# Scores of two pairs of heads in seven shared blocks, heads A and B on the two halves of TensorE's rows, and softmax's division moved to the output

## The chip, the cores and the metric

The kernel runs on one core of a Trainium2 chip. The metric is device microseconds of one execution, smaller is better. The core's engines are TensorE (PE; its weight loads stand apart as PEld), VectorE (DVE), ScalarE (ACT), GpSimd (POOL) and SyncE (SP, which here only issues DMAs). PSUM has eight banks of 128 x 512 f32.

## The reference, cut to what matters

Attention over 8 batches of 12 heads (448 tokens, 64 numbers each), then a gated MLP over each batch:

```
q_n, k_n = rmsnorm(q, g_q), rmsnorm(k, g_k)
scores   = (q_n @ k_n.T) / 8                 # 448 x 448 per head
attn     = exp(scores - max);  attn /= sum(attn) + 1e-9
x        = attn @ v                          # heads beside each other: 448 x 768 per batch
h        = gelu(x @ w_in);  u, w = halves of h
out      = x + (u * (w_sg @ layernorm(w) + b_sg)) @ w_out
```

All inputs are float32 or float64. The kernel gets float32 precision out of 16-bit matmuls: it splits each operand into a high float16 part and a low one (what the high part leaves over) and adds up the products of the parts.

## The kernel before, in words

The work goes through 48 pairs of heads, A and B (six pairs a batch). A pair has 2 x 448 = 896 rows of scores in seven tiles of 128 rows by 448 keys. Three tiles are A's, three are B's, and the middle one holds 64 rows of each.

For each pair: `load_qk` brings q and k of two pairs by eight DMAs, on ACT's queue (L269). `squares` (ACT square L324, DVE sum L325) and `norms` (DVE, small operands, L335 and L107 to L118) make the RMS factors. `split` multiplies by them on POOL (L344, L345), takes the high part on ACT (L347) and the low one on POOL (L348), copies k's parts with high and low swapped (DVE L350, L351), and one DMA transpose (SP, L352) makes `qt`. In `qt` the 128 partitions are 64 high and 64 low numbers of one head, so two matmuls with all 128 rows of TensorE (L411) give high x high + low x low, and high x low + low x high.

`scores` then does, for each tile: the maximum (DVE L414) on the scores in a PSUM bank; the exponential (ACT L416) from PSUM into a float32 tile `a` in SBUF, which also sums the row; for every two or three tiles a scale and a reciprocal of the sums (DVE L420, L422); the high part of `a` times the reciprocal on POOL (L430, three tiles of seven, four in the first batch) or ACT (L432, the rest); the low part on DVE (L433); and, for two tiles at a time, a DMA transpose into `at` (SP, L436). A PSUM bank of scores is free as soon as L416 has read it; there are four of them (NS), and three for the MLP (NM) and one for pv (NV).

`vsplit` makes v's high and low part (ACT L384, DVE L386), `vsquares` the sums for v's scale (ACT L367). `pv` of the pair before multiplies (L453 for 384 query columns, L455 for the other 64): A's matmuls use columns 0 to 63 of TensorE and B's columns 64 to 127. Eleven steps of four matmuls, then `xh` (ACT L461) and `xl` (DVE L462). `moe` is the MLP of the batch before: L517 and L520 (v half), L575 (u half), L605 (over tokens), L639 to L651 (output); gelus stand in clusters between two loads of ACT's table (L471, L480). The output goes out on ACT's queue (L658 to L661).

The order on each engine is set at build time: the main loop (L709 to L764) takes steps of `scores`, `pv`, the weights and `moe` in turn, and a list scheduler places the instructions by priority. Engines take their instructions in that order.

Of the kernel before, what the change touches and what calls it, by code (L numbers as in the profile page):

```python
# [44 lines left out]
def kernel(  # L45
# [28 lines left out]
    C7 = 2 * CM + 1  # L74
    EH = DM // 2
# [34 lines left out]
    def newton(y, x, t):  # L110
        """y, a guess of x ** -0.5 within 3.5%, made better by a step of third and one of second order."""
# [41 lines left out]
    def weights():  # L153
        nonlocal mlp
        ctx_w = ExitStack()
        # w_in's parts take the place of its float32 values, one K block after the other
# [49 lines left out]
        for c in range(CM):  # L206
            nc.sync.dma_start(out=wsr[c], in_=w_sg[0:SM].rearrange("(p c) s -> p c s", c=CM)[:, c])
# [489 lines left out]
    for i in range(NG):  # L697
        squares(i)
        norms(i, 1)
        if i == 0:  # L700
            split(0, V)
# [94 lines left out]
```

## Time and profile before

| | |
|---|---|
| Time, three runs | 1047.78, 1049.43 (median), 1049.59 us |
| Profiled execution, first to last instruction (span) | 1047.2 us; 2.2 us under the median |
| Busy: DVE, PE, ACT, POOL | 899.9, 809.6, 705.4, 504.6 us |
| The same as shares of the span | 86%, 77%, 67%, 48% |
| Mean granted clock of TensorE | 0.903 of full speed |
| DMA packets, bytes | 528217, 177.74 MB |

A row of the groups view reads: line of the kernel, engine, operation, tile written <- tiles read, shape (partitions x elements), count | busy time of the group in us, mean ns of one | idle time of the engine just before them and what ended it. Busy time of a group is the time in which at least one of them ran, so matmuls, which overlap, have a sum of means above their busy time. "PE s L411 <- ACT a L416: 63.5, 40, 7.9" in the view of waits says that L411 waited 63.5 us in 40 waits, 7.9 the longest, and that L416 ended those waits. In a timeline row the first number is the start in us, the second the length. Profile lines before carry line numbers of the kernel before.

### The profile page before, as it was taken

What the parts mean: (1) busy time and instruction counts of PE and PEld (TensorE: products, weight loads), DVE (VectorE), ACT (ScalarE), POOL (GpSimd) and SP (SyncE); (2) the same over time, 40 slices, a digit from 0 to 9 for tenths busy, and PEclk for the clock granted to TensorE, in tenths of its full rate; (3) what the DMA queues carried; (4) which work ended last, traced back from release to release, by engine and by line L of the source; (5) the groups of instructions that cost most, each with busy time, mean ns of one, the idle gap of its engine ahead of it and who ended that gap; (6) DMA issues with size and microseconds to landing.
All of it is one profiled execution on the core that took longest, in us unless ns stands there. A gap on an engine that the chain in (4) does not pass through costs nothing. (4 is left out here: it accounts for less than half of the span.)

```text
span 1047.2 us, 17092 instructions
## 1 busy us (share of the span) xinstructions
PE 809.6 (77%) x5652; PEld 447.3 (43%) x5652; DVE 899.9 (86%) x1959; ACT 705.4 (67%) x1418; POOL 504.6 (48%) x435
## 2 busy tenths in 40 slices
PE   0333556757689798888979899887979799799998
PEld 0111222424454346444644357343634365346546
DVE  4999979999789997999979998999889988999430
ACT  2565787676677777677767767587667686877441
POOL 1777745637536463443545372545455443535021
PEclk9666688888899899899999899999989999999999
DMA  5969589685989979996797879994989779838501
GB/s 144 254 174 244 125 179 215 160 185 108 207 180 206 194 156 206 173 217 152 162 213 181 167 149 196 202 211 106 207 190 195 148 166 201 180 89 174 110 1 61
DMA packets 528217, 177.74 MB, mean 170 GB/s; under 512 B 472257, under 2 KB 521985, under 8 KB 528129
## 3 DMA queue, kind: packets, MB, share of 16 engines
q1 hardware_dynamic: 484928, 144.07, 66.6%
q10 hardware_dynamic: 43200, 32.59, 11.3%
q8 instruction: 44, 0.72, 0.3%
q14 instruction: 45, 0.36, 0.1%
HBM read 54.58 MB, written 11.01 MB: 63 GB/s over the span
## 5 line engine op out<-in xcount | busy, mean ns | idle before, releaser
L433 DVE SCALAR_TENSOR_TENSOR ahl<-a,rc,ahl 128x448 f16<-128x448 f32 x336 | 289.6, 886 | 32.1 <-POOL ahl L430 22.0
L416 ACT ACTIVATE a<-s,nm 128x448 f32<-128x448 f32 x336 | 211.0, 630 | 124.7 <-DVE ahl L433 78.0
L411 PE MATMUL s<-qt 128*128 128x448 f16 (+1 forms) x768 | 192.2, 388 | 120.8 <-ACT a L416 63.5
L430 POOL TENSOR_SCALAR ahl<-a,rc 128x448 f16<-128x448 f32 x150 | 117.3, 786 | 230.0 <-DVE rc L422 99.9
L414 DVE TENSOR_REDUCE nm<-s 128x1 f32<-128x448 f32 x336 | 200.2, 610 | 18.5 <-PE s L411 18.0
L432 ACT ACTIVATE ahl<-a,rc 128x448 f16<-128x448 f32 x186 | 118.1, 662 | 61.5 <-DVE rc L422 34.2
L411 PEld LDWEIGHTS <-qt 128*128 128x128 f16 (+1 forms) x768 | 57.2, 105 | 209.2 <-issue 127.8
L345 POOL TENSOR_TENSOR qk<-qk,ny 128x896 f32<-128x896 f32 x47 | 83.2, 1792 | 70.6 <-DVE ny L118 34.4
L348 POOL TENSOR_TENSOR hl<-qk,hl 128x896 f16<-128x896 f32 x47 | 95.7, 2037 | 34.4 <-ACT hl L347 26.3
L453 PE MATMUL pv<-at,vl 128*64 128x384 f16 x384 | 68.2, 368 | 56.7 <-DMA at<-ahl 44.8
L344 POOL TENSOR_TENSOR qk<-qk,gg 128x448 f32<-128x448 f32 x47 | 58.9, 1255 | 77.0 <-ACT sqk L324 76.8
L453 PE MATMUL pv<-at,vh 128*64 128x384 f16 x672 | 91.0, 357 | 0.0
L575 PEld LDWEIGHTS <-wi 128*128 128x128 f16 x576 | 57.4, 102 | 61.8 <-issue 15.9
L455 PE MATMUL pv<-at,vh 128*64 128x64 f16 x672 | 78.7, 202 | 0.0
L611 POOL TENSOR_TENSOR gt<-gt,u 128x448 f32<-128x448 f32 x32 | 39.0, 1221 | 79.0 <-DVE gt L610 59.2
L453 PEld LDWEIGHTS <-vl 128*64 128x64 f16 x384 | 30.7, 118 | 90.0 <-DMA at<-ahl 37.0
L416 ACT ACTIVATION_READ_ACCUMULATOR a<-s,nm 128x1 f32 x336 | 65.9, 196 | 0.0
L325 DVE TENSOR_REDUCE ss<-sqk 128x14 f32<-128x896 f32 x48 | 51.5, 1073 | 15.5 <-ACT sqk L324 15.2
L347 ACT ACTIVATE hl<-qk 128x896 f16<-128x896 f32 x48 | 45.3, 945 | 25.6 <-DMA qk<-in_k_dram 11.4
L324 ACT ACTIVATE sqk<-qk 128x896 f32<-128x896 f32 x48 | 45.3, 944 | 21.7 <-DVE ss L325 11.2
L453 PEld LDWEIGHTS <-vh 128*64 128x64 f16 x672 | 50.2, 120 | 18.6 <-issue 0.8
L420 DVE TENSOR_SCALAR rc<-sums 128x2 f32<-128x2 f32 x144 | 52.1, 364 | 7.1 <-ACT a L416 6.5
(995 smaller groups left out, 2096.0 us busy)
## 6 DMA issues: line engine op xcount, KB each, us to landing
qk<-in_k_dram ACTq DMA_DIRECT2D x48, 192.0 KB, 3.6
vr<-in_v_dram SPq DMA_DIRECT2D x16, 576.0 KB, 4.9
vr<-in_v_dram SPq DMA_DIRECT2D x32, 288.0 KB, 5.9
out_dram<-ot ACTq DMA_DIRECT2D x24, 384.0 KB, 3.8
qk<-in_q_dram ACTq DMA_DIRECT2D x46, 192.0 KB, 3.6
raw<-in_moe_w_in_dram SPq DMA_DIRECT2D x12, 512.0 KB, 4.9
vr<-in_v_dram SPq DMA_DIRECT2D x32, 96.0 KB, 4.9
at<-ahl SPq DMA_TRANSPOSE x192, 3.8
```

The costliest lines, as they stand in the source:

```text
L344: E.tensor_tensor(out=qk[:, C7:], in0=qk[:, C7:], in1=gg.unsqueeze(1).broadcast_to([P, C7, D]), op=ALU.mult)
L345: E.tensor_tensor(out=qk, in0=qk, in1=r["rs"].unsqueeze(2).broadcast_to([P, SSW, D]), op=ALU.mult)
L348: E.tensor_tensor(out=hl[:, 0:SSW, 1], in0=qk, in1=hl[:, 0:SSW, 0], op=ALU.subtract)
L411: mm(out=ps[p0:p1], lhsT=qt[:, t * P + p0:t * P + p1], rhs=qt[:, k0:k0 + S], start=(n == 0), stop=(n == 1))
L414: V.tensor_reduce(out=nm, in_=ps, axis=AX.X, op=ALU.max, negate=True)
L416: A.activation(out=a, in_=ps, func=AF.Exp, bias=nm, accum_out=sums[:, t - t0:t - t0 + 1])
L430: G.tensor_scalar(out=hl[:, 0], in0=a, scalar1=sc, scalar2=1.0, op0=ALU.mult, op1=ALU.mult)
L432: A.activation(out=hl[:, 0], in_=a, func=AF.Copy, scale=sc)
L433: V.scalar_tensor_tensor(out=hl[:, 1], in0=a, scalar=sc, in1=hl[:, 0], op0=ALU.mult, op1=ALU.subtract)
L453: mm(out=o[:, 0:SM].rearrange("p (c n) -> p c n", c=CM), lhsT=w, rhs=at[:, h * CK:h * CK + CM, blk], start=(n == 0), stop=(n == n_s - 1), ...
L455: mm(out=o[:, SM:S], lhsT=w, rhs=at[:, CM, blk, h * HP:(h + 1) * HP], start=False, stop=(n == n_s - 1), skip_group_check=True)
L575: done = mm(out=ps[:, 0:S], lhsT=ww[:, g, f * P:(f + 1) * P], rhs=xx, start=(n == 0), stop=(n == 17))
```

## The change: what it does

The unit of the scores is now two pairs of heads (24 units). Tokens are laid out so that seven blocks of 128 rows hold both pairs: blocks 0 to 2 and the lower half of block 3 are pair 0, the rest is pair 1. A block has 64 numbers of head A beside 64 of head B; q's high, q's low, k's high and k's low part are four such sets. After the transposes (two per unit, q and k apart) A's numbers lie on partitions 0 to 63 and B's on 64 to 127. A tile of scores is 128 rows of both heads: A's matmuls take the lower half of TensorE's rows into one PSUM bank and B's the upper half into a second, three products each (high x high, low x high, high x low). So a unit has 7 tiles of 896 numbers a row, 168 in all, where there were 336 of 448.

Per tile there is one maximum over both banks (L392), two exponentials that write back into PSUM (L394), one high part for both heads on ACT (L397, none on POOL), one low part on DVE (L398), both read from PSUM, and one DMA transpose (L403; two of 64 rows where the ring of `at` wraps). The two banks are free only after L398; there are two such pairs of banks (NS = 2). The parts are no longer divided by the sum. Instead `recips` (per pair) adds 1e-9 on POOL, takes the reciprocal on DVE, splits it on POOL, spreads it over 64 partitions by 16 small matmuls against an identity (L423), copies that out on ACT (L426); and `pv` multiplies its output by it on DVE (L450). `pv` has twelve steps of two matmuls over all 448 columns. v is loaded without its duplicates. All loads of q and k and the output's stores are on SP's queue now, in halves of 64 partitions. In the last batch's MLP two tiles of the v half go block by block along with the heads, where it was three.

```diff
-RG = ((0, 2), (2, 4), (4, 7))
-TG = (2, 2, 2, 1)
-PT, PT0 = (0, 3, 6), (0, 2, 4, 6)
...
-NS, NV, NM = 4, 1, 3
...
-NA, NAH, NAT, NQT, NVH, HLB = 4, 4, 2, 2, 2, 2
+NS, NV, NM = 2, 1, 3
...
+NAT, NAH, NQT, NVH, HLB, GV = 3, 3, 2, 2, 3, 3
...
-        qs = qs or [nc.scalar]
+        qs = qs or [nc.sync]
...
+        qk = ld.tile([P, 2, 2, C7, D], F32, name="qk", bufs=NQK)
         for x, src in enumerate((q, k)):
...
+            for half, j, b0, c0, n in ((lo, 0, 0, 0, C4), (hi, 0, 0, C4, CM), (lo, 1, C4, C4, CM), (hi, 1, CM, 0, C4)):
+                qs[nq % len(qs)].dma_start(
...
-    def split(i, E=G):
...
-        V.tensor_copy(out=hl[:, SSW:, 0], in_=hl[:, C7:SSW, 1])
-        V.tensor_copy(out=hl[:, SSW:, 1], in_=hl[:, C7:SSW, 0])
-        r["tr"] = nc.sync.dma_start_transpose(out=qt, in_=hl.rearrange("p c x d -> p (c x d)"))
...
+    def split(u, E=G):
...
+        qt = att.tile([P, 4, C7 * P], F16, name="qt", bufs=NQT)
+        for x in range(2):
...
+            A.activation(out=h_, in_=r["qk"][:, x], func=AF.Copy)
+            E.tensor_tensor(out=l_, in0=r["qk"][:, x], in1=h_, op=ALU.subtract)
+            r["tr"] = nc.sync.dma_start_transpose(
...
-    def scores(i):
...
-                for n in range(2):
-                    for p0, p1, h in parts:
-                        k0 = (2 * (n + 1) + h) * S
-                        mm(out=ps[p0:p1], lhsT=qt[:, t * P + p0:t * P + p1], rhs=qt[:, k0:k0 + S],
-                           start=(n == 0), stop=(n == 1))
...
-                A.activation(out=a, in_=ps, func=AF.Exp, bias=nm, accum_out=sums[:, t - t0:t - t0 + 1])
...
+    def scores(u):
...
+        for t in range(C7):
+            ps = ps_s.tile([P, 2, 512], F32, name="s")
+
+            rows = [(slice(0, P), t // C4)] if t != CM else [(lo, 0), (hi, 1)]
+            for m, (qx, kx) in enumerate(((0, 2), (1, 2), (0, 3))):
+                for h in range(2):
+                    hs = slice(h * HP, (h + 1) * HP)
+                    for r_, j in rows:
+                        mm(out=ps[r_, h, 0:S], lhsT=qt[hs, qx, t * P + r_.start:t * P + r_.stop],
+                           rhs=qt[hs, kx, j * S:(j + 1) * S], start=(m == 0), stop=(m == 2))
+            nm = sml.tile([P, 2], F32, name="nm", bufs=6)
+            V.tensor_reduce(out=nm, in_=ps[:, :, 0:S], axis=AX.X, op=ALU.max, negate=True)
+            for h in range(2):
+                A.activation(out=ps[:, h, 0:S], in_=ps[:, h, 0:S], func=AF.Exp, bias=nm[:, h:h + 1], accum_out=sums[:, t, h:h + 1])
+            yield
+            ahl = att.tile([P, 2, 2, S], F16, name="ahl", bufs=NAH)
+            A.activation(out=ahl[:, 0], in_=ps[:, :, 0:S], func=AF.Copy)
+            V.tensor_tensor(out=ahl[:, 1], in0=ps[:, :, 0:S], in1=ahl[:, 0], op=ALU.subtract)
...
+    def recips(i):
...
+        G.tensor_scalar(out=x, in0=sums, scalar1=1e-9, scalar2=None, op0=ALU.add)
+        V.reciprocal(out=y, in_=x)
+        G.tensor_copy(out=rh, in_=y)
+        G.tensor_tensor(out=rl, in0=y, in1=rh, op=ALU.subtract)
...
+                    mm(out=ps[h * HP:(h + 1) * HP, o:o + w], lhsT=rx[ks, 2 * n + h:2 * n + h + 1].broadcast_to([w, HP]),
+                       rhs=ident_h[ks, ks], start=(n == 0 and rx is rh), stop=(n == CM and rx is rl), skip_group_check=True)
+        row = att.tile([P, S], F32, name="row", bufs=1)
+        A.activation(out=row, in_=ps, func=AF.Copy)
...
+        for k_, (vx, n, hx) in enumerate(blocks):
+            for h, (ks, c) in enumerate(hx):
+                mm(out=ps[h * HP:(h + 1) * HP], lhsT=vx[ks, c], rhs=at_all[ks, n + c, o:o + S],
...
+        V.tensor_tensor(out=ps, in0=ps, in1=row, op=ALU.mult)
...
-                nc.scalar.dma_start(out=om[t], in_=ot)
...
+            for h in range(2):
+                nc.sync.dma_start(out=om[1][t + h * C4] if t < CM else om[h][CM], in_=ot[h * HP:(h + 1) * HP])
```

On ACT, a stretch in a middle batch of the kernel before, while the MLP's gated tiles (`gh`) are made: `a` is an exponential, `ahl` the high part; "waits" names the engines whose semaphores the instruction waits for.

```order
L416 ACTIVATE a_5528,sums_5501<-s_5523,nm_5526 128x448 [waits DVE_49]
L612 ACTIVATE gh_5329<-gt_5401 128x448 [waits Pool_49]
L416 ACTIVATE a_5606,sums_5599<-s_5601,nm_5604 128x448 [waits DVE_49]
L416 ACTIVATE a_5627,sums_5599<-s_5620,nm_5625 128x448 [waits DVE_49,PE_49]
L432 ACTIVATE ahl_5573<-a_5528,rc_5502 128x448 [waits DMAHW5_49,DVE_49,Activation_49]
L432 ACTIVATE ahl_5638<-a_5606,rc_5600 128x448 [waits DMAHW6_49,DVE_49,Activation_49]
L416 ACTIVATE a_5673,sums_5666<-s_5668,nm_5671 128x448 [waits DVE_49]
```

The same place in the changed kernel: `s` is the pair of banks, written back by its two exponentials.

```order
L394 ACTIVATE s_5956,sums_5802<-s_5956,nm_5963 128x448 [waits DVE_49]
L369 ACTIVATE vh_6065<-vr_5248,v_s_5409 128x448 [waits PE_49]
L394 ACTIVATE s_5956,sums_5802<-s_5956,nm_5963 128x448 [waits Activation_49]
L453 ACTIVATE xh_6029<-pv_5897 128x448 [waits DVE_49]
L397 ACTIVATE ahl_5987<-s_5956 128x896 [waits DMAHW3_49,Activation_49]
L605 ACTIVATE gh_6147<-gt_6235 128x448 [waits Pool_49]
L394 ACTIVATE s_5999,sums_5802<-s_5999,nm_6012 128x448 [waits DVE_49]
```

Before, ACT waits for DVE ahead of an exponential and the high parts lag; now a tile's two exponentials and its high part stand close together, and the second exponential and the high part wait for ACT's own earlier work.

On SP, the DMAs of about a pair and a half of heads in the kernel before (`vr` is v, `at` the transposed weights of attention, `qt` the transposed q and k), all transposes but for the end of a load of v:

```order
L307 DMA vr_4260<-in_v_dram 64x6x64 [waits DMAHW5_49]
L307 DMA vr_4260<-in_v_dram 64x6x64 [waits DMAHW6_49]
L436 DMA_TRANSPOSE at_4271<-ahl_4323 128x14x128 [waits DMAHW2_49,DVE_49,DMAHW7_49,PE_49,Pool_49]
L436 DMA_TRANSPOSE at_4271<-ahl_4408 128x14x128 [waits DMAHW1_49,DVE_49,Pool_49]
L436 DMA_TRANSPOSE at_4271<-ahl_4478 128x7x128 [waits DMAHW2_49,DVE_49]
L436 DMA_TRANSPOSE at_4271<-ahl_4460 128x14x128 [waits DMAHW3_49,DVE_49]
L352 DMA_TRANSPOSE qt_4508<-hl_4505 128x21x128 [waits DMAHW5_49,DVE_49,PE_49]
```

And of the changed kernel, loads of q and k and stores of the output among the transposes:

```order
L403 DMA_TRANSPOSE at_97<-ahl_2740 128x14x128 [waits DMAHW7_49,DVE_49]
L651 DMA out_0_dram<-ot_2726 64x768 [waits DMAHW0_49,Activation_49]
L651 DMA out_0_dram<-ot_2726 64x768 [waits DMAHW1_49]
L403 DMA_TRANSPOSE at_97<-ahl_2793 128x14x128 [waits DMAHW2_49,DVE_49]
L278 DMA qk_3086<-in_q_dram 64x2x256 [waits DMAHW3_49,Pool_49]
L278 DMA qk_3086<-in_q_dram 64x2x192 [waits DMAHW4_49]
L278 DMA qk_3086<-in_q_dram 64x2x192 [waits DMAHW5_49]
L278 DMA qk_3086<-in_q_dram 64x2x256 [waits DMAHW6_49]
L278 DMA qk_3086<-in_k_dram 64x2x256 [waits DMAHW7_49]
L278 DMA qk_3086<-in_k_dram 64x2x192 [waits DMAHW0_49]
L278 DMA qk_3086<-in_k_dram 64x2x192 [waits DMAHW1_49]
L278 DMA qk_3086<-in_k_dram 64x2x256 [waits DMAHW2_49]
```

What stood on ACT's queue (q, k, output) now stands between the transposes of the scores on SP's.

More of the change, by code (lines that the diff above doesn't have):

```diff
@@ L74 @@
     C7 = 2 * CM + 1
+    C4 = CM + 1
+    NG = 2
+    NU = NP // NG
     EH = DM // 2
@@ L96 @@
     make_identity(nc, ident)
+    ident_h = const.tile([P, P], F16, name="ident_h")
+    A.activation(out=ident_h, in_=ident, func=AF.Copy)
     swap = const.tile([P, P], F32, name="swap")
@@ new lines, in squares, with norms @@
+        V.tensor_reduce(out=SS[u][:, x], in_=skv, axis=AX.X, op=ALU.add)
+    def norms(u):
+        n = 2 * SSW
+        ss = SS[u].rearrange("p a b -> p (a b)")
+        x, t = (sml.tile([P, n], F32, name=f"n{c}", bufs=2) for c in "xt")
+        si = sml.tile([P, n], I32, name="ni", bufs=2)
+        y = sml.tile([P, n], F32, name="ny", bufs=3)
+        V.tensor_scalar(out=x, in0=ss, scalar1=1.0 / D, scalar2=1e-6, op0=ALU.mult, op1=ALU.add)
+        rsqrt_guess(y, si, x)
+        newton(y, x, t)
+        U[u]["rs"] = y
@@ new lines @@
+    at_all = att.tile([P, 2 * C7, NAT * S], F16, name="at", bufs=1)
+    def scores(u):
+        qt = U[u]["qt"]
+        sums = sml.tile([P, C7, 2], F32, name="sums", bufs=2)
+        U[u]["sums"] = sums
+        for t in range(C7):
[15 more added lines that the diff above has]
+            V.tensor_tensor(out=ahl[:, 1], in0=ps[:, :, 0:S], in1=ahl[:, 0], op=ALU.subtract)
+            src = ahl.rearrange("p x h n -> p (x h n)")
+            o = (NG * u * S + t * P) % (NAT * S)
+            for r_ in ([slice(0, P)] if o + P <= NAT * S else [lo, hi]):
+                o1 = (o + r_.start) % (NAT * S)
+                nc.sync.dma_start_transpose(out=at_all[:, :, o1:o1 + r_.stop - r_.start], in_=src[r_])
+            yield
@@ L617, in moe @@
         idn = VS[b]["idn"]
-        om = out[b, 0:SM].rearrange("(p c) e -> c p e", c=CM)
+        om = [out[x].rearrange("(p c) e -> c p e", c=C7) for x in (b - b % 2, b)]
         A.activation(out=gth[:, :, half], in_=gh[:, :, SM:S].bitcast(F32), func=AF.Copy)
@@ L695 @@
     V.scalar_tensor_tensor(out=gg, in0=gg, scalar=0.125, in1=gk_b, op0=ALU.mult, op1=ALU.mult)
[L697 to L701, printed above, removed]
-    for i in range(2, 2 * NQK, 2):
-        load_qk(i)
-    first = R[0]["tr"].ins
+    for x in range(2):
+        squares(0, x)
+    norms(0)
+    split(0, V)
+    first = U[0]["tr"].ins
+    load_qk(1)
     load_v(0)
+    load_qk(2)
     with tc.issue_after(first):
@@ L708 @@
             load_v(i * GV)
+    sc = None
     for i in range(NI + 1):
         b, g = divmod(i, NP)
-        if i < NI and i % NG == 0 and i + NG < NI:
-            for j in range(NG):
-                squares(i + NG + j)
-            norms(i + NG, NG)
-        if i + 1 < NI:
-            split(i + 1)
-        if i < NI and i % 2 == 1:
-            load_qk(i - 1 + 2 * NQK)
+        u = i // NG
+        if i == 0:
+            for x in range(2):
+                squares(1, x)
+            norms(1)
+        if i < NI and i % NG == 0 and i + NG < NI:
+            split(u + 1)
+            load_qk(u + 1 + NQK)
+        if i % NG == 1 and i + NG + 1 < NI:
+            for x in range(2):
+                squares(u + 2, x)
+            norms(u + 2)
         if i < NI:
@@ L760 @@
         for s_, n_ in streams:
-            if s_ is not pend and s_ is not wts:
+            if s_ is not pend and s_ is not wts and (s_ is not sc or i % NG == 1):
                 drain(s_)
```

252 lines of the change are left out of this document (93 added, 159 removed).

## The prediction

> **What bounds the kernel now.** First the page's busy times, then the stretches: the start (loads, no scores yet), the body with scores and weights, and the end, where only the last batch's MLP is left. The columns are busy time of PE, PEld, DVE, ACT and POOL with their instructions, the granted clock, the DMA engines' share and GB/s.
>
> ```profile
> span 1047.2 us, 17092 instructions
> 0.00:50.00 50.00, 10.25 (x30) 3.33 (x31) 34.55 (x76) 20.26 (x38) 20.55 (x22) 0.85 0.81 198
> 50.00:950.00 900.00, 710.88 (x5005) 387.50 (x5006) 827.34 (x1798) 640.45 (x1294) 464.80 (x390) 0.90 0.83 178
> 950.00:1047.20 97.20, 88.48 (x623) 56.42 (x619) 37.98 (x88) 44.72 (x88) 19.28 (x25) 0.99 0.34 79
> ```
>
> In the body DVE works 827.3 of 900 us, 92%. PE has 79%, the DMA engines 83%, ACT 71%, POOL 52%. DVE sets the pace, and what others wait for is DVE above all:
>
> ```profile
> ACT a L416 <- DVE ahl L433: 78.0, 80, 4.7
> ACT ahl L432 <- DVE rc L422: 34.2, 32, 3.0
> PE s L411 <- ACT a L416: 63.5, 40, 7.9
> ```
>
> The third row is PE waiting for a bank of scores to come free, with four banks. So the sum is made engine by engine: which is fullest after the change, and how full can it get.
>
> **DVE.** Its groups that the change touches, and with them POOL's share of the high parts:
>
> ```profile
> L433 DVE SCALAR_TENSOR_TENSOR ahl<-a,rc,ahl 128x448 f16<-128x448 f32 x336 | 289.6, 886 | 32.1 <-POOL ahl L430 22.0 <-ACT ahl L432 10.1
> L414 DVE TENSOR_REDUCE nm<-s 128x1 f32<-128x448 f32 x336 | 200.2, 610 | 18.5 <-PE s L411 18.0
> L420 DVE TENSOR_SCALAR rc<-sums 128x2 f32<-128x2 f32 x144 | 52.1, 364 | 7.1 <-ACT a L416 6.5
> L325 DVE TENSOR_REDUCE ss<-sqk 128x14 f32<-128x896 f32 x48 | 51.5, 1073 | 15.5 <-ACT sqk L324 15.2
> L462 DVE SCALAR_TENSOR_TENSOR xl<-pv,xh 128x448 f16<-128x448 f32 x48 | 29.3, 610 | 9.5 <-ACT xh L461 9.5
> L351 DVE COPY hl<-hl 128x448 f16<-128x448 f16 x48 | 25.4, 531 | 0.1
> L422 DVE RECIPROCAL rc<-rc 128x2 f32<-128x2 f32 x144 | 22.6, 160 | 1.4
> L350 DVE COPY hl<-hl 128x448 f16<-128x448 f16 x48 | 15.6, 325 | 0.0
> L430 POOL TENSOR_SCALAR ahl<-a,rc 128x448 f16<-128x448 f32 x150 | 117.3, 786 | 230.0 <-DVE rc L422 99.9 <-ACT a L416 28.3 <-DVE rc L420 16.6
> ```
>
> Maximum and low part now take 896 numbers at a time. L414 and L325 give 610 ns for 448 and 1073 for 896; L462, a low part out of PSUM like the new one, has L414's 610 ns, so I take 1073 for both: 336 x 1.073 = 361 us for 289.6 + 200.2 = 490, or -129. The bounds are L433's 2 x 886 for the low part (+118) and 1073. I take the lower, since L462's operands are those of the new instruction (PSUM and SBUF) and L433's both lie in SBUF.
>
> Scale and reciprocals: -74.7, +48 x 0.16 = 8. Copies L350 and L351: -41. The multiplication on pv's output: +48 x 0.61 = 29. v's low part on 448 numbers for 512: -3. Sum -211; with about 5% of it outside the body, DVE there falls from 827 to some 627 us. POOL loses L430's 117 and gains 144 operations on eight numbers; at 465 us in the body it had room.
>
> One wait is new on DVE: the reciprocal waits for POOL's addition. Behind it in DVE's queue stand maxima and low parts, and PE's 16 matmuls wait for POOL's split after it. POOL's other operations of 786 ns and more can be in front; half of such a one, 48 times, is 19 us of DVE. DVE has room for that.
>
> **ACT.**
>
> ```profile
> L416 ACT ACTIVATE a<-s,nm 128x448 f32<-128x448 f32 x336 | 211.0, 630 | 124.7 <-DVE ahl L433 78.0 <-DVE nm L414 32.4 <-DVE rc L420 4.1
> L432 ACT ACTIVATE ahl<-a,rc 128x448 f16<-128x448 f32 x186 | 118.1, 662 | 61.5 <-DVE rc L422 34.2 <-issue 11.4 <-DVE nt L116 2.6
> L416 ACT ACTIVATION_READ_ACCUMULATOR a<-s,nm 128x1 f32 x336 | 65.9, 196 | 0.0
> L384 ACT ACTIVATE vh<-vr,v_s 128x896 f16<-128x896 f32 x48 | 49.6, 1035 | 6.8 <-DVE v_s L134 3.8 <-DMA at<-ahl 2.9
> L347 ACT ACTIVATE hl<-qk 128x896 f16<-128x896 f32 x48 | 45.3, 945 | 25.6 <-DMA qk<-in_k_dram 11.4 <-DVE ss L325 5.3 <-DMA qt<-hl 4.5
> L461 ACT ACTIVATE xh<-pv 128x448 f16<-128x448 f32 x48 | 25.6, 533 | 18.0 <-PE pv L455 17.7 <-PE s L411 0.2
> L367 ACT ACTIVATE sqv<-vr 128x1536 bf16<-128x1536 f32 x16 | 23.7, 1478 | 14.9 <-DMA vr<-in_v_dram 14.4 <-DMA qt<-hl 0.5
> L269 ACTq DMA_DIRECT2D qk<-in_k_dram x95: 374/602/1572, 0.7 to 892.9; - x95
> ```
>
> The exponentials stay 336 of 630 ns; writing PSUM is not shown, and I leave them between 533 (L461) and 662. All high parts are ACT's now: 168 of 896 numbers at L347's 945 ns (bounds 945 and twice L461, 1066) is 159 for 118. The reciprocal rows add 48 x 0.53 = 26. v's high part on half the numbers is 662 (L432's form) for 1035: -18; L367 on seven eighths: -3. Together +46, or 640 + 43 = 683 in the body.
>
> The second exponential and the high part now wait for ACT's own last result. A reading of the accumulator, 196 ns, then no longer overlaps what follows. I take 0.1 us of idle time for each of the 336, so 34 (bounds 0 and 0.2, 67). That makes 717. For it ACT no longer issues the loads of q and k (0.6 us each of its queue) and the stores; as it was only 71% full I count nothing for that (bounds: a gain up to 188 x 0.6 = 113 of queue time, and no loss).
>
> **PE.** Back-to-back matmuls of 448 columns start 0.19 us apart; the two of pv for A and B run beside each other, both with their 64-column ones in the same 0.19. Changing to 64 rows and back shows as 0.29 and 0.28:
>
> ```profile
> 930.00 0.34 PE L453 MATMUL pv<-at,vh 128*64 128x384 f16 x2
> 930.19 0.34 PE L453 MATMUL pv<-at,vh 128*64 128x384 f16 x2
> 933.82 0.35 PE L605 MATMUL ms__11321<-ws_l,vh 128*128 128x448 f16 x1
> 934.01 0.35 PE L605 MATMUL ms__11293<-ws_h,vl 128*128 128x448 f16 x1
> 934.30 0.36 PE L605 MATMUL ms__11293<-ws_h,vh 64*128 64x448 f16 x1
> 934.50 0.35 PE L605 MATMUL ms__11293<-ws_l,vh 64*128 64x448 f16 x1
> 934.78 0.36 PE L605 MATMUL ms__11321<-ws_h,vl 128*128 128x448 f16 x1
> L411 PE MATMUL s<-qt 128*128 128x448 f16 (+1 forms) x768 | 192.2, 388 | 120.8 <-ACT a L416 63.5
> L455 PE MATMUL pv<-at,vh 128*64 128x64 f16 x672 | 78.7, 202 | 0.0
> ```
>
> If row halves run beside each other as column halves do, a tile of both heads is three steps: 168 x (3 x 0.19 + 0.17 for the last to drain) = 124 for L411's 192, or -68. pv has a twelfth step: 48 x 0.19 = +9. The 768 small matmuls of the reciprocals fit four to a 0.19 step like pv's small ones, 0.05 each, +38 (bound: L455's 202 ns, 155). Two changes of the rows in use per tile, 0.1 each: +34 (bounds 0, 34). So 711 + 13 = 724. The Trainium skill (TensorEngine Tiling (Array Packing), section "Key Properties") speaks for and against: different tiles of the array can load weights and multiply in parallel, but changing the tiling mode drains the array. The trace bears out the first for columns and the second in the 0.1 per change; for row halves no run here shows the first. By the rule PE's sum stays 724, without it it is 820.
>
> **DMA and SP.**
>
> ```profile
> q1 hardware_dynamic: 484928, 144.07, 66.6%
> q10 hardware_dynamic: 43200, 32.59, 11.3%
> L436 SPq DMA_TRANSPOSE at<-ahl x192: 1221/1482/6457, 44.3 to 979.3; - x192
> L352 SPq DMA_TRANSPOSE qt<-hl x48: 2614/2931/6055, 23.2 to 945.8; - x48
> ```
>
> The scores' transposes move what they moved. qt falls by a third (33 MB by its shape to 22), v by half (22 to 11): 155 of 177 MB, or 816 us of engine time to about 715. On SP, issuing took 192 x 1.48 + 48 x 2.93 = 425 us for transposes by the medians; now 176 x 1.48 + 48 x 1.48 = 332, and 188 loads and some 60 stores at 0.6 add 150: 482 (v's loads stay about as many). Neither is full, so both count nothing; a transpose behind eight loads comes 4.8 us late, which three buffers of `ahl` cover (a tile every 4.8 us). Without that cover it is the fourth rival.
>
> **The sum.** After the change ACT is fullest (717), PE beside it (724 with its draining), DVE at 627. DVE now gets to 92%. Two engines close to their ends disturb each other more, so I choose 0.89, the middle between DVE's 0.92 and a 0.86 in which the idle share nearly doubles: body 717 / 0.89 = 806 us. The start gains 3 (DVE splits twice as much for the first unit: 2240 more numbers at L325's rate), the end 4 (18 matmuls of the v half stay behind the last head). Span 806 + 147 + 7 = 960; with the 2.2 us by which the median exceeds the span, 962. Its own range, 0.92 to 0.86: 935 to 990. A difference under 0.2%, 2 us, counts as none.
>
> **The rivals.**
>
> Row halves one after the other: a tile takes six steps, not three, 168 x 3 x 0.19 = 96 us more, so PE has 820 in the body; at 0.92 that is 891, and 1047 in all. For it: nothing in the trace shows rows beside each other. Against it: columns do. Chance 0.12, on either side of no change.
>
> Slower: two pairs of banks are too few. A pair of banks is held from the first matmul to the end of the low part: 0.74 + 1.07 + 2 x 0.73 + 0.95 + 1.07 = 5.3 us of pure service, through five queues, where before it ended at the exponential. Now a tile of both heads takes 900 / 168 = 5.36 us, so with two pairs it decides from a round trip of 10.7 us, 5.4 of it waiting. At 11.3 the time is 168 x 5.65 + 156 = 1105. For it: PE waits 63.5 us for banks even with four. Against it: that came from DVE at 92%, which falls to 78%. Chance 0.10.
>
> Faster: ACT's own waits hide and it gets to 0.92: 683 / 0.92 + 156 = 898. For it: DVE gets that far now. Chance 0.12.
>
> SP's queue: loads and stores hold the transposes up. If 4.8 us per unit show for half of their 24 x 4.8, it is 962 + 58 = 1020. For it: SP blocks at each wait. Chance 0.08.
>
> The forecast has 0.58. Faster by over 0.2%: forecast 0.58, the fast one 0.12, SP 0.08, some 0.04 of the row halves: 0.82. The same 0.04, slower 0.14. The range 900 to 1045 leaves out the slow one, half of the fast one and a part of the row halves: 0.2.
>
> **What would show it.** In the profile of the changed kernel: L398 and L392 at 1.07 us, DVE near 690 us in all; ACT the fullest with some 750; starts of L389's A and B matmuls within a few ns, three steps of 0.19; waits of L389 for DVE's low part small. I am wrong if A's and B's matmuls start 0.19 apart, if L389 waits for L398 by over 100 us, if L403 waits behind L278, or if DVE still is the fullest.

## The result, and the profile after

The changed kernel takes 1036.74 us (median of 4 runs, 1033.44 to 1037.19) beside 1048.61 (4 runs, 1046.70 to 1049.59) of the kernel before: ratio 0.9884, interval 0.9867 to 0.9902. It is 1.2% faster where 8.3% was forecast. The direction was right, the size wrong.

The page's busy times and the same three stretches as before (PE, PEld, DVE, ACT, POOL with their instructions, granted clock, DMA share, GB/s):

```profile
span 1031.6 us, 16639 instructions
PE 829.0 (80%) x5844; PEld 421.1 (41%) x5844; DVE 733.3 (71%) x1332; ACT 738.1 (72%) x1449; POOL 386.9 (38%) x403
```

```profile
0.00:50.00 50.00, 9.43 (x60) 4.07 (x61) 30.07 (x59) 25.57 (x47) 14.78 (x19) 1.00 0.78 193
50.00:950.00 900.00, 752.55 (x5394) 379.00 (x5393) 683.76 (x1230) 684.25 (x1357) 361.44 (x370) 0.91 0.74 158
950.00:1031.60 81.60, 67.02 (x390) 38.05 (x390) 19.43 (x45) 28.26 (x47) 10.67 (x15) 0.92 0.18 43
```

DVE's 92% of the body are gone, and nothing has taken their place: PE has 84%, DVE and ACT 76% each. DVE's busy time went down by 167 us and the time by 12, so the engines wait for each other more. The groups that the change made, by busy time, mean, and idle time ahead of them:

```profile
L394 ACT ACTIVATE s<-s,nm 128x448 f32<-128x448 f32 x336 | 204.0, 607 | 109.8 <-DVE nm L392 106.8
L398 DVE TENSOR_TENSOR ahl<-s,ahl 128x896 f16<-128x896 f32 x168 | 182.1, 1085 | 100.8 <-ACT ahl L397 99.8
L389 PE MATMUL s<-qt 64*128 64x448 f16 (+1 forms) x1152 | 143.2, 390 | 110.7 <-DVE ahl L398 76.4
L392 DVE TENSOR_REDUCE nm<-s 128x2 f32<-128x896 f32 x168 | 180.8, 1082 | 40.5 <-PE s L389 40.0
L397 ACT ACTIVATE ahl<-s 128x896 f16<-128x896 f32 x168 | 153.4, 920 | 5.3 <-DMA at<-ahl 3.1
L423 PE MATMUL row<-ident_h,rh 128*64 128x128 f16 (+1 forms) x384 | 36.7, 240 | 31.7 <-POOL rh L415 24.0
L450 DVE TENSOR_TENSOR pv<-pv,row 128x448 f32<-128x448 f32 x48 | 30.0, 624 | 22.3 <-PE pv L446 22.0 <-PE mo__6671 L636 0.4
L426 ACT ACTIVATE row<-row 128x448 f32<-128x448 f32 x48 | 26.0, 542 | 6.5 <-PE row L423 6.3
```

Read the last columns as a ring: PE waits for DVE's low part (76.4), DVE's maximum for PE (40.0), ACT's exponentials for that maximum (106.8), DVE's low part for ACT's high part (99.8). Each step of a tile waits for the one before it, and the first step waits for the last step of an earlier tile. The chain of the page, in shares of the span, says the same: no engine carries it.

```profile
PE 34%; DVE 21%; ACT 19%; DMA 11%; issue 8%; SPq 4%; POOL 4%; ACTq 0%; POOLq 0%; DVEq 0%
```

Where the 15.6 us between the profiled spans (the medians are 11.9 apart) come from is seen in the first and the last issue of the scores' transposes, whose row for before (44.3 to 979.3) is in the prediction:

```profile
L403 SPq DMA_TRANSPOSE at<-ahl x176: 1229/1506/4939, 41.0 to 962.8; - x176
```

The stage of the scores went from 935 us to 922. What follows the last transpose is as long as before (67.9 and 68.8 us).

One stretch of the timeline (start, length; PE, ACT and DVE alone, some rows left out) shows how a wait is passed on:

```profile
605.28 1.09 DVE L392 TENSOR_REDUCE nm<-s 128x2 f32<-128x896 f32 x1 [0.86 <-PE s L389]
...
606.41 0.61 ACT L394 ACTIVATE s<-s,nm 128x448 f32<-128x448 f32 x1 [1.26 <-DVE nm L392]
...
607.16 0.61 ACT L394 ACTIVATE s<-s,nm 128x448 f32<-128x448 f32 x1
...
608.33 0.33 PE L644 MATMUL mo__6630<-wo_l,gth 128*128 128x384 f32 x1
608.50 0.34 PE L644 MATMUL mo__6630<-wo_h,gtl 128*128 128x384 f32 x1
...
608.88 0.49 ACT L648 ACTIVATE ot<-mo__6630 128x384 f32<-128x384 f32 x1 [0.99 <-PE mo__6630 L644]
609.00 0.74 PE L389 MATMUL s<-qt 64*128 64x448 f16 x5
609.26 0.91 ACT L397 ACTIVATE ahl<-s 128x896 f16<-128x896 f32 x1
...
610.21 1.09 DVE L398 TENSOR_TENSOR ahl<-s,ahl 128x896 f16<-128x896 f32 x1 [3.83 <-ACT ahl L397]
...
611.25 1.09 DVE L392 TENSOR_REDUCE nm<-s 128x2 f32<-128x896 f32 x1
...
612.38 0.61 ACT L394 ACTIVATE s<-s,nm 128x448 f32<-128x448 f32 x1 [2.20 <-DVE nm L392]
```

The tile's second exponential ends at 607.8, and its high part could follow. But ahead of the high part ACT's queue has a copy of the MLP's output, which waits 0.99 us for PE's output products. So the high part comes at 609.26, DVE's low part after 3.83 us of idle time, and the maximum of the next tile behind it in DVE's queue, for which ACT then waits 2.20 us. All that time the banks are held. A wait that starts with PE's work for the MLP went through ACT and DVE and came back.

The theory at this point: a tile's hold of its pair of banks, lengthened by whatever else stands in the three queues, sets the pace. The rivals: one engine alone still does (PE, with 84%); or it is the queue on which loads are issued. Over all tiles, the time from the end of one low part to the end of the low part two tiles later, which uses the same banks, is 11.1 us in the mean, 5.56 a tile. This round is twice the pace of the tiles by its making, whatever sets the pace. The hold is a part of it: from a tile's first matmul to the end of its low part the banks are held 9.6 us in the mean, and they stand free for the other 1.5.

### The profile page after: what moved, and what is told of

Its sections match the earlier page's. It is cut to its first block, busy times and chain, and to the rows that moved or that the text cites. A ratio compares the mean times of both kernels' runs of the same rounds, so it can differ in the third digit from the quotient of the medians.

```text
span 1031.6 us, 16639 instructions
## 1 busy us (share of the span) xinstructions
PE 829.0 (80%) x5844; PEld 421.1 (41%) x5844; DVE 733.3 (71%) x1332; ACT 738.1 (72%) x1449; POOL 386.9 (38%) x403
## 4 chain that ended last, share of the span: by engine, by line
PE 34%; DVE 21%; ACT 19%; DMA 11%; issue 8%; SPq 4%; POOL 4%; ACTq 0%; POOLq 0%; DVEq 0%
PE pv L446 6%; ACT s L394 5%; DVE ahl L398 5%; PE s L389 4%; DVE nm L392 3%; ACT ahl L397 2%; DMA vr<-in_v_dram 2%; ACT sqk L308 2%; DMA raw<-in_moe_w_in_dram 2%; DMA at<-ahl 2%; POOL qk L330 2%; DMA qt<-hl 2%; DMA qk<-in_k_dram 2%; ACT hl L334 2%; SPq L336 1%
## 5 line engine op out<-in xcount | busy, mean ns | idle before, releaser
L394 ACT ACTIVATE s<-s,nm 128x448 f32<-128x448 f32 x336 | 204.0, 607 | 109.8 <-DVE nm L392 106.8
L398 DVE TENSOR_TENSOR ahl<-s,ahl 128x896 f16<-128x896 f32 x168 | 182.1, 1085 | 100.8 <-ACT ahl L397 99.8
L389 PE MATMUL s<-qt 64*128 64x448 f16 (+1 forms) x1152 | 143.2, 390 | 110.7 <-DVE ahl L398 76.4
L392 DVE TENSOR_REDUCE nm<-s 128x2 f32<-128x896 f32 x168 | 180.8, 1082 | 40.5 <-PE s L389 40.0
L397 ACT ACTIVATE ahl<-s 128x896 f16<-128x896 f32 x168 | 153.4, 920 | 5.3 <-DMA at<-ahl 3.1
L446 PE MATMUL pv<-at,vh 128*64 128x448 f16 (+1 forms) x768 | 122.7, 398 | 16.4 <-DMA at<-ahl 7.6
L389 PEld LDWEIGHTS <-qt 64*128 64x128 f16 (+1 forms) x1152 | 45.3, 102 | 177.2 <-issue 135.9
L309 DVE TENSOR_REDUCE ss<-sqk 128x14 f32<-128x896 f32 x48 | 51.8, 1080 | 29.2 <-ACT sqk L308 28.9
L394 ACT ACTIVATION_READ_ACCUMULATOR s<-s,nm 128x1 f32 x336 | 67.7, 201 | 0.0
L329 POOL TENSOR_TENSOR qk<-qk,gg 128x896 f32<-128x896 f32 x23 | 48.0, 2085 | 43.2 <-ACT sqk L308 39.3
L423 PE MATMUL row<-ident_h,rh 128*64 128x128 f16 (+1 forms) x384 | 36.7, 240 | 31.7 <-POOL rh L415 24.0
L446 PE MATMUL pv<-at,vl 128*64 128x448 f16 (+1 forms) x384 | 60.4, 394 | 0.0
```

Of the source, the lines that this page charges most:

```text
L309: V.tensor_reduce(out=SS[u][:, x], in_=skv, axis=AX.X, op=ALU.add)
L389: mm(out=ps[r_, h, 0:S], lhsT=qt[hs, qx, t * P + r_.start:t * P + r_.stop], rhs=qt[hs, kx, j * S:(j + 1) * S], start=(m == 0), stop=(m == 2))
L392: V.tensor_reduce(out=nm, in_=ps[:, :, 0:S], axis=AX.X, op=ALU.max, negate=True)
L394: A.activation(out=ps[:, h, 0:S], in_=ps[:, h, 0:S], func=AF.Exp, bias=nm[:, h:h + 1], accum_out=sums[:, t, h:h + 1])
L397: A.activation(out=ahl[:, 0], in_=ps[:, :, 0:S], func=AF.Copy)
L398: V.tensor_tensor(out=ahl[:, 1], in0=ps[:, :, 0:S], in1=ahl[:, 0], op=ALU.subtract)
```

## The experiments

Ratios are to the kernel before, timed on the same chip beside the run; differences in us are (ratio - 0.9884) x 1049, that is, against the changed kernel, unless it says otherwise.

One thing holds for all of them. The order on each engine is set at build time, and with an edit it comes out differently: of ACT's 1044 instructions in the changed kernel, at most 747 stand in the same sequence (by operation and tile) in the run with the thin MLP, and 674 in the version with the exponentials in SBUF. No run holds the order fixed, so how much of a difference of a few us is the order's stays open.

**Where the exponentials go.** The first run writes them to an SBUF tile, so that the banks are free two steps earlier; the room came from one of three scratch buffers. The second takes away that scratch buffer alone.

```
-A.activation(out=ps[:, h, 0:S], in_=ps[:, h, 0:S], func=AF.Exp, ...)
+a = att.tile([P, 2, S], F32, name="a", bufs=2)
+A.activation(out=a[:, h], in_=ps[:, h, 0:S], func=AF.Exp, ...)      # L397, L398 read a
-HLB = 3
+HLB = 2                                                            # alone in the second run
```

> The exponentials write a float32 tile in SBUF again (two such tiles, and two in place of three buffers of the shared scratch to make room), so a pair of banks is free after the exponential. Ring theory (two pairs of banks set the pace: the round trip of 11.1 us, measured from one end of the low part to the next on the same banks, gives 5.56 us a tile): the round trip loses the waits and lengths of high and low part, 0.83 + 0.92 + 0.52 + 1.08 = 3.35 us, so the ring alone would allow 3.9 us a tile and the engines bind: ACT about 690 us in the body at 0.85 to 0.9, in all 920 to 970 us. TensorE theory (PE, 84% of the body and 91% between 300 and 450 us, sets the pace): 1025 to 1045. Order theory (the engines' fixed orders make them wait for each other wherever the slack is): 1005 to 1030. Against all: the low part has two SBUF operands again and can cost up to 30 us more of DVE.

> The changed kernel with two buffers of the shared scratch in place of three, as the run with the exponentials in SBUF needs it: its control. All theories: within 1% of the changed kernel, 1030 to 1047 us.

1038.06 us, ratio 0.9882 (0.9856 to 0.9909), and 1067.58, ratio 1.0152 (1.0114 to 1.0190). So a scratch buffer is worth 28 us, and the banks' shorter hold 28 (0.027 of 1049) against this control. What the missing scratch buffer does stands in the row of the squares of q and k on ACT, in the run with two:

```profile
L308 ACT ACTIVATE sqk<-qk 128x896 f32<-128x896 f32 x48 | 45.7, 951 | 28.1 <-DMA qt<-hl 21.7 <-DMA qk<-in_q_dram 3.4 <-issue 1.7
```

ACT stands still for 21.7 us until a transpose of q and k has read its buffer, and all exponentials behind it with it. In the changed kernel no such wait is in that row.

**A third pair of banks.** PSUM has room for it only if the MLP has one bank; the first run is the changed kernel with that alone, the second with the third pair. All tiles of the MLP are then copied out of PSUM, and the last batch's v half is no longer done early.

```
-NS, NV, NM = 2, 1, 3
+NS, NV, NM = 2, 1, 1        # second run: 3, 1, 1
-VC, UC = (3,), (0, 1)
+VC, UC = (0, 1, 2, 3), (0, 1, 2, 3)
```

> The MLP lives in one PSUM bank in place of three (each of its tiles is copied out by ACT; no tiles that go along with the heads), two pairs of banks for the scores as in the change: the control of the run with three pairs. ACT has some 8 x 5 x 0.6 = 24 us more, PE waits for its one bank. Ring theory: 1040 to 1080. TensorE theory: 1050 to 1100, since PE stalls at each change of the bank.

> As the run with the MLP in one bank, but with three pairs of banks for the scores. Ring theory: the pace goes from 11.1 / 2 to 11.1 / 3 = 3.7 us a tile and the engines bind; 60 to 110 us less than with two pairs. TensorE theory: PE has the same work, within 10 us of two pairs. Order theory: 10 to 40 us less.

1114.86 us, ratio 1.0606 (1.0570 to 1.0643), and 1106.82, ratio 1.0525 (1.0494 to 1.0556). The third pair gave 8 us. The scores' last transpose came at 972.6 instead of 998.7. A pair of banks was held 14.4 us in the mean instead of 9.9, so the tiles came at nearly the same pace (one every 5.6 us instead of 5.8). 2.6 us of the longer hold lie between the exponentials and the high part; for that one's own buffers ACT waited 28.6 us in all, 3.3 with two pairs. That speaks against the hold as the one cause: with a slot more, the waits grew to fill it. As the MLP with one bank makes its own waits (the end after the last transpose grew from 69 to 110 and 135 us), this pair doesn't settle it.

**Work added to and taken from one engine.** Each adds work whose result is not used, ahead of each tile's maximum (DVE, ACT) or in pv (PE); the fourth takes matmuls from the MLP.

```
+V.tensor_reduce(out=jd, in_=<gg, 7 x 64>, axis=AX.X, op=ALU.max)     # DVE
+A.activation(out=ja, in_=<gg, 7 x 64>, func=AF.Copy)                 # ACT
+for _ in range(8): <two matmuls of pv's last block>                  # PE
-for xx, ww in ((xh, wi_h), (xl, wi_h), (xh, wi_l)):                  # thin MLP, likewise v half and tokens
+for xx, ww in ((xh, wi_h),):
```

> An extra maximum over 448 numbers ahead of each tile's own maximum on DVE (its result is not used): 168 x 0.61 = 102 us more of DVE. DVE has 684 of 900 us in the body of the changed kernel. If DVE is the bound the time rises by about 102 us (1139). If only the busiest engine counts and that is PE, by less than 20. If the engines wait for each other in a fixed order (coupling), by part of it, 30 to 60 us, with the wait of PE's L389 for DVE's low part (76 us) growing. If the round trip of a tile on its two pairs of banks sets the time, 0.61 is added to a round of 11.1 wherever DVE is not idle before the maximum: half of 168 x 0.61, about 50, and less if the added one runs while DVE would wait for the tile.

> An extra copy of 448 numbers ahead of each tile's maximum in the program, on ACT (its result is not used): 168 x 0.55 = 92 us more of ACT, which has 684 of 900 us in the body. If ACT is the bound, +92 (1129). If PE is, less than 20. Coupling: 30 to 60. Round trip: as the copy waits for nothing, it can fill ACT's idle time before the first exponential (1 to 2.6 us), then 0 to 30.

> Eight more steps of two matmuls per pair of heads at the beginning of pv on PE, whose sums are overwritten by the regular steps: 48 x 8 x 0.19 = 73 us more of PE, which has 753 of 900 us in the body. If PE is the bound, +73 (1110). If ACT or DVE is, less than 15. Coupling: 20 to 45. Round trip: the added matmuls stand between two tiles' scores and delay one of seven tiles by 1.5 us, 24 x 2 x 1.5 at most halved by the other pair of banks, up to 36.

> The MLP's v half, u half and token products keep only high x high and leave the two products with a low part out (the output products stay whole): two thirds of those matmuls go, about 150 to 200 us of PE of which 30 in the end after the last head. ACT, DVE and POOL do what they did. If PE is the bound, the body shrinks by over 100 us and the next bound is ACT with 684: 900 or less. If only the tile's round trip or ACT and DVE's order sets the pace, the body stays and only the end gains: 1000 to 1015. Coupling with PE as one of three: 930 to 980.

The rows of the work added to DVE and to ACT, from their two profiles:

```profile
L392 DVE TENSOR_REDUCE jd<-gg 128x7 f32<-128x448 f32 x168 | 96.9, 605 | 0.0
```

```profile
L392 ACT ACTIVATE ja<-gg 128x448 f16<-128x448 f32 x168 | 97.4, 580 | 2.0 <-DVE gg L687 0.8
```

More DVE: 1077.16, ratio 1.0243 (1.0197 to 1.0290), 38 us for 97 of work; records of an engine overlap, and DVE's busy time as a whole grew by 65 (798.0 for 733.3). More ACT: 1070.13, ratio 1.0185 (1.0122 to 1.0248), 32 for 97, by which its busy time grew by 78 (816.1 for 738.1). More PE: 1058.13, ratio 1.0069 (1.0044 to 1.0094), 19 for the 57 by which PE's busy time grew. So a microsecond of busy time more shows by 0.58 on DVE, 0.41 on ACT and 0.34 on PE: none is the bound, and none is free.

The thin MLP: 1027.52, ratio 0.9770 (0.9728 to 0.9813), 12 us less. Its page's busy times, its body, and PE's wait for banks:

```profile
span 1027.1 us, 14428 instructions
PE 698.3 (68%) x4724; PEld 354.4 (35%) x4724; DVE 748.0 (73%) x1332; ACT 744.8 (73%) x1451; POOL 384.4 (37%) x403
```

```profile
50.00:950.00 900.00, 635.87 (x4360) 318.72 (x4359) 695.09 (x1226) 685.87 (x1349) 357.44 (x366) 0.79 0.73 158
```

```profile
PE s L389 <- DVE ahl L398: 119.9, 48, 8.9
```

PE lost 131 us of busy time and the kernel 12: PE alone is not the bound. The wait of its first matmuls for banks grew from 76 to 120 us, so a third of what was freed went straight into that wait. And the scores gained nothing:

```profile
L403 SPq DMA_TRANSPOSE at<-ahl x176: 1238/1497/5551, 39.4 to 962.5; - x176
```

Their last transpose comes at 962.5 us, in the changed kernel at 962.8. What this profile gains lies behind it (64.6 us for 68.8).

**The division left out.**

```
-row = recips(i)
-V.tensor_tensor(out=ps, in0=ps, in1=row, op=ALU.mult)
```

> The division is left out altogether (no recips, no copy of the row, no multiplication on pv's output), so the output is not divided by the sums. It takes 48 x (0.54 + nothing else) = 26 us off ACT, 48 x (0.62 + 0.19) = 39 off DVE, 71 off PE (both groups of small matmuls) and the waits for POOL's two small operations. If each engine's work shows by the shares that the added work showed (0.35, 0.38, 0.28), 9 + 15 + 20 = 44 us: 993. If the reciprocals lie beside other work, under 10 us: over 1027. If the wait for POOL holds PE's queue up, more than 44.

1032.33, ratio 0.9844 (0.9814 to 0.9874): 4 us, with intervals that overlap, where I had worked out 44 from the added work. Work taken away shows by much less than work added. Moving the division to the output was cheap.

**The queue of the loads.** The changed kernel with loads and stores back on ACT's queue, and the kernel before with them on SP's.

```
-qs = qs or [nc.sync]             # changed kernel
+qs = qs or [nc.scalar]
-nc.sync.dma_start(out=om[...], in_=ot[...])
+nc.scalar.dma_start(out=om[...], in_=ot[...])
...
-qs = qs or [nc.scalar]           # kernel before, the stores likewise
+qs = qs or [nc.sync]
```

> The loads of q and k and the stores of the output go back to ACT's queue, as in the kernel before; the rest is the changed kernel. If ACT's time is as short as the other engines', 188 + 62 issues of some 0.6 us show by a third: 40 to 50 us slower (1080). If loads and stores on SP's queue hold the transposes up (my fourth rival), 10 to 30 us faster. If neither, within 10 us.

> The kernel before with one part of the change alone: loads of q and k and stores of the output on SP's queue. If ACT's queue time counts there as it does in the changed kernel (63 us for 145), 123 us of issuing leave it and the kernel gains 30 to 50: 1000 to 1020, and the rest of the change is then a loss. If DVE with 92% is the bound there, within 10 us of 1049; then the move only pays together with the rest. If loads hold up the transposes, slower.

1099.52, ratio 1.0492 (1.0459 to 1.0525): 64 us slower. The issues on ACT's queue in that run, by minimum, median and maximum in ns, and ACT's busy time in the body:

```profile
L278 ACTq DMA_DIRECT2D qk<-in_q_dram x94: 602/628/1063, 0.7 to 837.9; - x94
L278 ACTq DMA_DIRECT2D qk<-in_k_dram x94: 602/618/1801, 2.4 to 840.6; - x94
L651 ACTq DMA_DIRECT2D out_dram<-ot x56: 472/503/762, 287.9 to 1098.4; - x56
```

```profile
50.00:950.00 900.00, 702.42 (x4906) 348.17 (x4906) 637.15 (x1160) 641.70 (x1265) 353.43 (x351) 0.87 0.76 151
```

188 x 0.62 + 56 x 0.50 = 145 us of ACT's queue that no busy time shows. If the 64 us are theirs alone, they cost 0.44 of themselves; PE's wait for the scores' transposes grew too, from 7.6 to 23.3 us. Without the move of the loads the change would be a loss of 5%.

The kernel before with that part alone: 1070.62, ratio 1.0222 (1.0192 to 1.0253), 23 us slower, not a gain. The expectation had put a loss down to loads that hold up the transposes, but PE waited less for those of q and k (41.3 us for 51.8) and of the scores (17.5 for 44.8). So the move pays only with the rest of the change. In that run the mean of DVE's low part rose from 886 to 943 ns and PE's wait for banks from 63.5 to 93.1; why the loads' place does this was not tried and stays open.

**How much the number of banks does.** The changed kernel with one pair, and the kernel before with two banks instead of four.

```
-NS, NV, NM = 2, 1, 3
+NS, NV, NM = 1, 1, 3
...
-NS, NV, NM = 4, 1, 3        # kernel before
+NS, NV, NM = 2, 1, 3
```

> The changed kernel with one pair of banks for the tiles instead of two. The work alone along a tile's round is 0.74 + 1.08 + 0.79 + 0.61 + 0.92 + 1.08 = 5.2 us, with the median gaps between the steps some 3 more. If the hold of the banks is all that sets the pace, a tile every 8 to 9 us: 1450 to 1600. If other work fills the gaps and the round shrinks as fast as its number of pairs, 1150 to 1300.

> The kernel before with two banks for its tiles instead of four. A bank is held for 7.4 us in the mean there, of which 2 are work; a tile comes every 2.68. If buffers between the engines are what let DVE fill to 92%, the hold falls to some 5 us and two banks give a tile every 2.5 to 3.5 us: 1100 to 1250 us. If DVE's work alone sets the pace, within 15 us of 1049.

One pair: 1457.64, ratio 1.3917 (1.3869 to 1.3965). Waits of the one-pair run:

```profile
ACT s L394 <- DVE nm L392: 250.7, 113, 5.2
PE s L389 <- DVE ahl L398: 242.3, 58, 11.8
DVE ahl L398 <- ACT ahl L397: 220.0, 125, 5.5
DVE nm L392 <- PE s L389: 169.9, 105, 4.6
```

It is the same ring. A tile comes every 8.1 us in the mean, and the banks are held 7.0 of them. The second pair brings 8.1 down to 5.56 a tile, not to 4.05, as each pair is then held 9.6 us: 2.6 us more of waiting. The kernel before with two banks: 1148.14, ratio 1.0982 (1.0939 to 1.1025), 103 us slower with the same work, and DVE's share of the span falls from 86% to 77%. So DVE's 92% of the body hung on the four banks.

**Four scratch buffers.** The step from two to three was worth 28 us.

```
-HLB = 3
+HLB = 4
```

> Four scratch buffers for three (HLB; squares of q, k and v, and the high and low parts of q and k before their transposes). From two to three the time fell by some 30 us. If the preparation of q and k still holds ACT's queue up, another 5 to 15 us faster (1022 to 1032). If three is enough, and the rest of the time lies in the order between tiles, within 3 us of the changed kernel (1037).

1040.13, ratio 0.9918 (0.9889 to 0.9947): 4 us slower, with intervals that overlap. Three are enough.

**A version faster than both.** The exponentials to SBUF, with all three scratch buffers; 11 instead of 12 buffers of xh and xl make room.

```
+a = att.tile([P, 2, S], F32, name="a", bufs=2)      # as in the first run
-NX = 12
+NX = 11
```

> The exponentials to SBUF again, now with the three scratch buffers of the changed kernel (room comes from 11 instead of 12 buffers of xh and xl). The pair of banks is free after the second exponential. If the pace is the tile's hold of its banks together with the order of the queues, the 29 us by which the first such run beat its own control come on top of the changed kernel: 1005 to 1015 (0.96 of the kernel before). If two scratch buffers were the only thing that the first run and its control had in common and the gain lay in easing them, nothing: 1030 to 1040. If ACT's or DVE's work is what counts, 1030 to 1050, as their work does not fall.

1013.82 us, ratio 0.9677 (0.9651 to 0.9703), in 5 runs: 22 us (2.1%) faster than the changed kernel and 3.2% than before. The groups, the body, and the scores' transposes:

```profile
L399 DVE TENSOR_TENSOR ahl<-a,ahl 128x896 f16<-128x896 f32 x168 | 229.8, 1371 | 46.1 <-ACT ahl L398 45.0
L395 ACT ACTIVATE a<-s,nm 128x448 f32<-128x448 f32 x336 | 209.5, 632 | 95.1 <-DVE nm L392 73.6 <-DVE nx L317 6.0 <-DVE ahl L399 5.3
```

```profile
50.00:950.00 900.00, 766.86 (x5442) 386.09 (x5441) 726.60 (x1238) 684.31 (x1370) 416.76 (x372) 0.92 0.75 161
```

```profile
L404 SPq DMA_TRANSPOSE at<-ahl x176: 1229/1528/4649, 41.5 to 922.9; - x176
```

DVE has 37 us more to do in all (769.8 for 733.3; the low part takes 1371 ns for 1085) and an exponential takes 25 ns more, and still the scores take 881 us for 922. More work with a shorter hold is faster: the hold was what counted. The 11 buffers of xh and xl have no run of their own. A part of the gain is lost again behind the last transpose, in the changed kernel and in this one:

```profile
962.80:1031.60 68.80, 58.77 (x352) 35.32 (x350) 13.03 (x38) 22.86 (x35) 10.04 (x12) 0.97 0.12 30
```

```profile
922.90:1010.70 87.80, 82.68 (x524) 53.81 (x522) 15.11 (x41) 27.58 (x45) 16.25 (x21) 1.00 0.17 42
```

172 more matmuls are left for the end, and it takes 19 us longer. (In the first run, with 12 of those buffers, the end takes 88.0 us as well.) So the shorter hold gains 40 us up to the last transpose and loses 19 after it. The Trainium skill (ScalarE: Activation LUTs, section "Step-by-step: what each stage is for") advises PSUM as the faster place for ScalarE's output, with the caveat that TensorE must not need most of PSUM. Both halves are in these rows: 607 ns to PSUM for 632 to SBUF, and the caveat decides.

**Both covers off.** The version just told, with the thin MLP.

> The exponentials to SBUF with three scratch buffers, and the MLP's v half, u half and token products keep only high x high (two products with a low part each are left out). If PE has become the bound with the exponentials in SBUF (612 of 650 us there), taking some 130 us of it away shows by half or more: under 950. If the queues' order still sets the pace, about 10 us as before: 1000.

964.53, ratio 0.9215 (0.9182 to 0.9248). Its span, the scores' transposes, and the stretch between the first and the last of them in the columns of before:

```profile
span 961.3 us, 14490 instructions
```

```profile
L404 SPq DMA_TRANSPOSE at<-ahl x176: 1230/1522/5125, 39.9 to 896.2; - x176
```

```profile
39.90:896.20 856.30, 607.49 (x4386) 311.38 (x4386) 738.08 (x1242) 688.26 (x1378) 415.88 (x375) 0.82 0.78 170
```

The four ratios of this square:

| | MLP whole | MLP thin |
|---|---|---|
| exponentials in PSUM | 0.9884 | 0.9770 |
| exponentials in SBUF | 0.9677 | 0.9215 |

The thin MLP takes 12 us off the changed kernel and 48 off the version with the shorter hold; the shorter hold takes 22 and, with the thin MLP, 58. Together they give 70 us, alone 12 + 22. Where these lie, by one profile each:

| | last transpose of the scores, us | from there to the end, us |
|---|---|---|
| changed kernel | 962.8 | 68.8 |
| thin MLP | 962.5 | 64.6 |
| exponentials in SBUF | 922.9 | 87.8 |
| both | 896.2 | 65.1 |

Up to the last transpose the thin MLP alone gains nothing, the shorter hold 40 us, and both 67. So there are two limits beside each other, the hold of the banks and the work in PE's queue: while the banks are held long, less work on PE does not show in the scores at all, and while PE has its whole work, a part of what the shorter hold gives does not show. Of the 48 us that the thin MLP takes off the version with the shorter hold, some 27 lie in the scores; the rest is work of the MLP that had been left for the end. With both eased DVE is busy for 738 of these 856 us, 86%; in the changed kernel it is 697 of 922, 76%. This is the strongest evidence for where the forecast gain went, and it shows why no probe of one of the two could find it.

## Why the prediction was wrong, step by step

**Most of the works were right to some per cent.** ACT: 683 us forecast in the body, 684.25 measured, with 607 ns for the exponential and 920 for the high part. That it fits so closely is in part luck: in all ACT has 33 us more than before (738.1 for 705.4), not 46, and a larger part of it lies in the body. The two new DVE groups: 361 forecast, 180.8 + 182.1 = 363 measured. The small reciprocal matmuls (both groups, rh and rl) took 71 us for 38, and L389 143 for 124; PE has 753 for 724. DVE in the body has 684, not 627. Its work fell as forecast: the busy times of its groups add up to 1010 us before and 790 after, 220 less where I had 211. But I took busy times of groups off the busy time of the engine. Groups overlap, by 110 us before and by 57 now, and so the engine's busy time fell by 167 only.

**Row halves beside each other: shown.** Six matmuls of a tile, three steps of two, in one entry:

```profile
500.59 0.74 PE L389 MATMUL s<-qt 64*128 64x448 f16 x6 [0.60 <-DVE ahl L398]
```

0.74 us is 3 x 0.19 + 0.17, and in the median A's and B's matmul start 4 ns apart. So the first rival (halves one after the other, 1047) is out, although its time was near the measured one, and the Trainium skill's rule that tiles of the array work in parallel (TensorEngine Tiling (Array Packing), section "Key Properties") holds here for rows.

**The step that failed: "so I choose 0.89, the middle between DVE's 0.92 and a 0.86".** I took the share to which the fullest engine gets as a property that carries over from one kernel to the next. ACT got to 0.76, PE to 0.84. DVE's 0.92 came with four banks, free after the exponential; the kernel before with two banks has DVE at 77% of the span instead of 86%. The change gave the tile two pairs of banks, free only after the low part. Freeing them after the exponentials gives back 22 of the 75 us by which the forecast missed, 40 up to the last transpose; for the rest the runs show only that the time falls further when PE's work is eased as well. It was also not ACT that was fullest: PE's own sum, 724, stood above ACT's 717, and by it the forecast would have been 970.

**The slower rival had the mechanism, and wrong ends.** It said that a pair held through five queues sets the pace, and the version with the shorter hold bears that out. Its bound, a round of 10.7 us, does not serve: a round is twice the pace by its making, and 10.7 came from 900 us where the scores took 935 before (11.1). And it did not come out at 168 x 5.56 + 156 = 1090, because the 156 us of ends counted time in which tiles already run: the first transpose goes out at 41.0, the last at 962.8. The same slip is in my 147: start and end around the scores were 44 + 68 = 112 before. I gave this rival 0.10 on the ground that PE's wait for banks had come from DVE at 92%. The wait did not go with DVE's load; it grew from 63.5 to 76.4 us.

**"I count nothing" for the loads that left ACT's queue was the largest error on a term of the works.** Put back, they cost 64 us. I read ACT as 71% full from busy time, which leaves out 0.6 us for each issue: with 188 of them in its queue it was nearer to 640 + 110, 83%. The bound I gave (a gain up to 113) held, the value taken did not. This error went the other way: with 64 us of gain counted the forecast would have been some 900. So it hid nearly half of what the fill of 0.89 had wrong, and that the miss is 75 us and not 139 is luck.

**SP's queue: right.** L403 behind L278 kept others waiting for some us only; pv waited 7.6 us for transposes in all. The reciprocals on POOL and DVE: right that they hide, as leaving them out gives 4 us.

**Of the signs named beforehand** that of the row halves and the 1.07 us of L392 and L398 (1082 and 1085 ns) came true. DVE near 690 us did not (733), nor ACT as the fullest with some 750 (738, below PE's 829). One sign of being wrong came true in part (L389 waits for L398 for 76 us, where I had set 100), and one that I had not named was the plainest: no engine near its end.

What stays open: why added work shows by a third to over a half and removed work by a tenth or less; the square shows one pair of such covers, but not whether there are others, and not what the order set at build time has in it. And why the kernel before loses with its loads on SP's queue.

## What to carry to other kernels

How full an engine can get belongs to the buffers around it, not to the engine: when a change takes buffers away or holds them over more steps, work out the round trip through all queues, with the other work that stands in them, before dividing work by an old fill. When one probe says that an engine isn't the bound, and another says it of the buffers, try both together: two limits that hide each other look like none. Read the gain by stage, as work can move from one stage into the next. Count DMA issues on a computing engine's queue as its work.

## What the runs showed of the hardware

- Taking matmuls away lowered TensorE's granted clock: mean 0.916 in the changed kernel, 0.805 with the thin MLP, 0.78 with one pair of banks; L389's mean went from 390 to 418 and 455 ns. The Trainium skill (TensorE: Matmul & The Clock Gate, section "What's actually happening") says that the clock follows how busy the array has been, and the runs agree. A probe that empties TensorE slows what is left on it.
- A subtraction of 128 x 896 on DVE took 1085 ns in the mean with one operand in PSUM and 1371 with both in SBUF (the version with the exponentials in SBUF). The medians are alike, 1091 and 1092: with both in SBUF, the 62 that ran beside no POOL instruction took 1085 in the mean and the 106 that ran beside one 1538, at most 2830; with one in PSUM POOL made no difference (1082 beside it, 1087 without).
- A DMA issue takes 0.60 to 0.63 us of ACT's or SP's queue for a load and 0.36 to 0.57 for a store, by the medians, and does not appear as busy time.
